# In-place weight conversion, more homes for weight blocks, and scores of three tiles in two row groups

## The chip, the cores and the metric

The kernel runs on one core of a Trainium2 chip. The metric is the device time of one execution in microseconds (us). Engines are TensorE (PE, with its weight loads PEld), VectorE (DVE), ScalarE (ACT), GpSimd (POOL) and SyncE (SP, which issues the DMAs).

## The reference

Local attention with a distance bias, followed by a gated channel mix. B, H, S, D = 4, 8, 768, 64; the model width is 512, the hidden width 1024.

```python
scores = scale * np.matmul(q, k.transpose(0, 1, 3, 2))
is_global = pos[None, :] < int(n_global)            # 8
is_local = (rel >= 0) & (rel < int(n_local))        # 96
dist = np.where(is_global & ~is_local, float(n_local), np.abs(rel))
scores = np.where(is_global | is_local, scores - slopes * dist, -1e9)
a = softmax(scores); x = a @ v                      # heads side by side: (4, 768, 512)
xk = mu_k * x + (1 - mu_k) * x_prev                 # xr likewise with mu_r
k = np.maximum(xk @ w_k, 0.0); v = k * k @ w_v
out = v / (1 + np.exp(-(xr @ w_r)))
```

The three weight matrices come as 64-bit floats; the rest as 32-bit floats.

## The kernel before, in words

**Tiles and steps.** The 3072 rows are 24 tiles of 128 queries, six for each batch. Step n does the scores of tile n, pair of heads by pair of heads (hp = 0 to 3), the transposes of tile n - 1 and the weighted sum over v of tile n - 2. A tile sees its own 128 keys and 128 earlier ones (the first tile of a batch only its own). Two tiles make a chunk of 256 rows; the channel mix of a chunk, an "FFN", is a generator whose pieces (`yield`) are dealt out between the pairs by `run_ffn`, five for each pair. FFN 0 is queued in step 3 with a budget of -17.5, so that its first matmuls stand in program order at that step's end.

**Scores.** Tiles 0 to 6 (`n < NATIVE`) use native 32-bit matmuls, later ones a high and a low part (L323, L324). A head has 64 rows. In the native tiles each query tile (`padded`, four buffers) has zeros in the other 64 rows, so that heads 0 to 3 (rows 0 to 63) and 4 to 7 (rows 64 to 127) go through all 128 rows of the array against `ring`, which holds the keys of both halves (L320 earlier keys, L321 own keys). The scores of one pair are in one PSUM buffer of a pool of two (`ps_s`). DVE adds the bias and takes the row's extreme (L332), ACT takes the exponential (L333), DVE sums and inverts (L339, L340), POOL scales (L343). Results lie in `room`, 12 slots.

**Weights.** There are 20 blocks of 128 x 512: 8 of w_k, 4 of w_r, 8 of w_v. A block is a DMA of 512 KB (L160), one multiplication on ACT or POOL by turns (L175, L173), and three integer passes on DVE (L176, L177, L178) which make 32-bit words of the two halves of a 64-bit number. The intermediate `a` has a place of its own, and the result goes into a `word` (pool `wl`, 21 buffers). The raw blocks lie in homes that others need later or earlier: w_k k=0 and k=1 in kk_hi and kk_lo, k=2 in xk_hi, k=3 in xr_hi, each for both column halves in turn; w_r and w_v in the three buffers `t4k`, with `a` in pool f2. kk_hi also holds the setup's temporary, and xk_hi, xr_hi, kk_hi receive the inputs (L429, L430) and the hidden values (L480) of FFN 0.

**FFN 0 and the others.** FFN 0 multiplies with the words as they are (`kp` L471, `z` L450, `vps` L507). For FFN 1 and later each word is split into a high part (`w_hi`, a copy on ACT or POOL) and a low part (DVE, L187 or L190), and each product has three matmuls (L441 to L443). `splits_ok` says how many blocks may be split, and one is split for each piece of FFN that is dealt.

**Order.** The program order is written out by hand in the loop over steps; after each pair a rule gives the number of weight loads and conversions that are due (`due`), and conversions are held behind the last score instructions of the pair before (`marks`, filled from `seen`). A planner then orders each engine's queue by program order and by its own simulated time; the queues are worked off in order.

Of the kernel before, what the change touches and what calls it, by code (L numbers as in the profile page):

```python
# [24 lines left out]
NATIVE = 7  # L25
MOVED = 9
# [7 lines left out]
def tile_biased_attention_channel_mix(ctx: ExitStack, tc: tile.TileContext, qT, kT, v, n_sizes, mu_kr, w_k, w_v, w_r, q_rows, k_rows, v_rows, slopes, out):  # L34
# [108 lines left out]
    w_steps = [(name, src, k, c) for name, src, kts, n in (("k", w_k, 4, DF), ("r", w_r, 4, DM), ("v", w_v, 8, DM)) for c in range(0, n, 512) for k in ((1, 2, 3, 0) if name == "k" else range(kts))]  # L143

    w_raw = {}

    def weight_load(i):
        name, src, k, c = w_steps[i]
        if name != "k":
            raw = p4k.tile([128, 512, 2], I32, tag="t4k", name=f"w64_{i}")  # L150
            a = f2_pool.tile([128, 512], I32, tag="f2", name=f"wa_{i}")
        elif k < 2:
            both = f_pool.tile([128, 2048], I32, tag=("kk_hi", "kk_lo")[k], name=f"w64_{i}")
            raw = both[:, 0:1024].rearrange("p (n w) -> p n w", w=2)
            a = both[:, 1024:1536]
        else:
            t = "xk" if k == 2 else "xr"
            raw = f_pool.tile([128, 512, 2], I32, tag=t + "_hi", name=f"w64_{i}")
            a = f_pool.tile([128, 512], I32, tag=t + "_lo", name=f"wa_{i}")
        nc.sync.dma_start(raw.rearrange("p n w -> p (n w)"), src[k * 128 : (k + 1) * 128, 2 * c : 2 * c + 1024])  # L160
        w_raw[i] = raw, a

    def weight_begin(i):
        name, src, k, c = w_steps[i]
        raw, a = w_raw.pop(i)
# [3 lines left out]

        if i % 2:
            pool.tensor_scalar(a.bitcast(F32), top.bitcast(F32), 2.0**-112, 1.0, op0=ALU.mult, op1=ALU.mult)  # L173
        else:
            act.mul(a.bitcast(F32), top.bitcast(F32), 2.0**-112)  # L175
        vec.tensor_scalar(a, a, 3, 0x7FFFFFF8, op0=ALU.logical_shift_left, op1=ALU.bitwise_and)  # L176
        vec.scalar_tensor_tensor(a, top, -0x80000000, a, op0=ALU.bitwise_and, op1=ALU.bitwise_or)  # L177
        vec.scalar_tensor_tensor(word, low, 29, a, op0=ALU.logical_shift_right, op1=ALU.bitwise_or)  # L178
# [58 lines left out]
    def load_tile(n):  # L237
        b, t = divmod(n, NT)
        s = state[n] = {}
        if n < NATIVE:  # L240
            qr, kr = padded[n % 4], ring[:, n % 4]
            for o, h in sides:
                nc.sync.dma_start(qr[o : o + 64, h : h + HH], qT[n, :, h : h + HH])
# [64 lines left out]
    def scores(n, hp):  # L308
# [5 lines left out]
        ps = ps_s.tile([128, 512], F32, name=f"s_{n}_{hp}", tag="s")  # L314
        for u in range(2):
            h = 2 * hp + u
            o = ps[:, u * 256 : u * 256 + w]
            if n < NATIVE:
                if t:
                    pe.matmul(o[:, 0:128], s["qr"][:, h, :], state[n - 1]["kr"][:, h % HH, :], start=True, stop=True)  # L320
                pe.matmul(o[:, w - 128 : w], s["qr"][:, h, :], s["kr"][:, h % HH, :], start=True, stop=True)  # L321
            else:
                pe.matmul(o, s["qh"][:, h, :], s["kw"][:, h, c0:256], start=True, stop=False)  # L323
                pe.matmul(o, s["ql"][:, h, :], s["kw"][:, h, c0:256], start=False, stop=True)  # L324
        if hp == 3 and n + 1 < NATIVE and (n + 1) % NT >= 2:
            vec.tensor_copy(s["kr"][:, :, 0:32], firsts)
        for u in range(2):
            h = 2 * hp + u
            o = ps[:, u * 256 : u * 256 + w]
            slot = 5 + (4 * (n - MOVED + 3) + 3 + hp) % 7 if n < MOVED - 2 else 8 + hp  # L330
            e = room[:, slot, 256 * u : 256 * u + 256]
            vec.tensor_tensor_reduce(out=e[:, :w], in0=o, in1=p[:, h, :], op0=ALU.add, op1=ALU.min, scale=-0.125, scalar=3.0e38, accum_out=s["nmax"][:, h : h + 1])  # L332
            seen["act"] = act.activation(e[:, :w], e[:, :w], AF.Exp, bias=s["nmax"][:, h : h + 1], scale=-1.0, accum_out=s["sum"][:, h : h + 1]).ins  # L333
            s["e"][h] = e
        if hp % 2 == 0:
            return
        h0, nh = 2 * hp - 2, 4
# [419 lines left out]
```

## Time and profile before

| | us |
|---|---|
| median of 3 runs | 490.45 (488.69 to 490.99) |
| the profiled execution | 487.47 |
| its span in the trace | 485.6 |
| PE busy | 471.2 |
| DVE busy | 379.2 |
| ACT busy | 280.1 |
| POOL busy | 254.3 |

A row of busy times is for one engine or one stretch. In a timeline, a line merges instructions of one kind: its start, its length, how many, and in brackets the idle time of the engine ahead of them with what released it. Matmuls overlap in the pipeline, so the distance between starts, not the length, tells what one occupies.

### The profile page before, as it was taken

What the parts mean: (1) busy time and instruction counts of PE and PEld (TensorE: products, weight loads), DVE (VectorE), ACT (ScalarE), POOL (GpSimd) and SP (SyncE); (2) the same over time, 40 slices, a digit from 0 to 9 for tenths busy, and PEclk for the clock granted to TensorE, in tenths of its full rate; (3) what the DMA queues carried; (4) which work ended last, traced back from release to release, by engine and by line L of the source; (5) the groups of instructions that cost most, each with busy time, mean ns of one, the idle gap of its engine ahead of it and who ended that gap; (6) DMA issues with size and microseconds to landing.
All of it is one profiled execution on the core that took longest, in us unless ns stands there. A gap on an engine that the chain in (4) does not pass through costs nothing.

```text
span 485.6 us, 9692 instructions
## 1 busy us (share of the span) xinstructions
PE 471.2 (97%) x3300; PEld 405.5 (84%) x3300; DVE 379.2 (78%) x921; ACT 280.1 (58%) x654; POOL 254.3 (52%) x396
## 2 busy tenths in 40 slices
PE   7997999999999999999999999999999999999996
PEld 6786855597898898898898898898898898898985
DVE  6899599898867978978988978978978968846321
ACT  5996345445658746645856746745748648544220
POOL 7677446735847535746646655637646635403000
PEclk9998999999999999999999999999999999999999
DMA  6994457331442464783685786683775655430001
GB/s 170 300 328 126 131 173 179 87 115 45 107 111 67 138 198 137 213 269 110 178 237 167 208 245 174 207 238 130 196 210 186 196 171 167 141 126 12 33 2 48
DMA packets 42279, 76.20 MB, mean 157 GB/s; under 512 B 5616, under 2 KB 23280, under 8 KB 42224
## 3 DMA queue, kind: packets, MB, share of 16 engines
q1 hardware_dynamic: 42080, 75.52, 52.6%
q8 instruction: 28, 0.46, 0.4%
q14 instruction: 27, 0.22, 0.2%
q10 hardware_dynamic: 144, 0.00, 0.0%
HBM read 54.53 MB, written 20.97 MB: 155 GB/s over the span
## 4 chain that ended last, share of the span: by engine, by line
PE 78%; DVE 10%; DMA 5%; issue 2%; POOL 2%; ACT 2%; SPq 0%; DVEq 0%; POOLq 0%
PE vps L442 8%; PE vps L441 8%; PE vps L443 8%; PE kp L441 8%; PE kp L443 8%; PE kp L442 8%; PE av L401 7%; PE z L441 4%; PE z L442 4%; PE s L323 4%; PE z L443 4%; PE s L324 3%; DMA w<-in_w_v_dram 2%; PE t L380 1%; DMA ring<-in_kT_dram 1%
## 5 line engine op out<-in xcount | busy, mean ns | idle before, releaser
L343 POOL TENSOR_SCALAR room<-room,r 128x256 f32<-128x256 f32 (+1 forms) x192 | 108.0, 579 | 131.7 <-DVE r L340 65.4
L333 ACT ACTIVATE room<-room,nmax 128x256 f32<-128x256 f32 (+1 forms) x192 | 92.8, 484 | 90.2 <-DVE nmax L332 84.2
L441 PE MATMUL kp<-xk_hi,wk_hi 128*128 128x256 f32 x352 | 99.5, 283 | 0.7 <-ACT xk_hi L420 0.7
L443 PE MATMUL kp<-xk_hi,wk_lo 128*128 128x256 f32 x352 | 98.6, 280 | 0.0
L442 PE MATMUL kp<-xk_lo,wk_hi 128*128 128x256 f32 x352 | 98.3, 279 | 0.0
L332 DVE CUSTOM_DVE_ANT_0 room<-s,pat 128x256 f32<-128x256 f32 (+1 forms) x192 | 68.5, 388 | 3.9 <-PE s L321 2.5
L442 PE MATMUL vps<-wv_lo,kk_hi 128*128 128x512 f32 (+1 forms) x184 | 70.9, 385 | 0.0
L441 PE MATMUL vps<-wv_hi,kk_hi 128*128 128x512 f32 (+1 forms) x184 | 70.8, 385 | 0.0
L443 PE MATMUL vps<-wv_hi,kk_lo 128*128 128x512 f32 (+1 forms) x184 | 70.5, 383 | 0.0
L441 PEld LDWEIGHTS kp<-xk_hi,wk_hi 128*128 128x128 f32 x352 | 66.8, 190 | 1.8 <-ACT xk_hi L420 1.0
L442 PEld LDWEIGHTS kp<-xk_lo,wk_hi 128*128 128x128 f32 x352 | 66.0, 187 | 0.8 <-issue 0.2
L443 PEld LDWEIGHTS kp<-xk_hi,wk_lo 128*128 128x128 f32 x352 | 66.0, 188 | 0.0
L354 DVE STREAM_TRANSPOSE room<-room 128x512 f32<-128x512 f32 x52 | 36.0, 702 | 17.9 <-POOL room L343 17.9
L486 DVE TENSOR_TENSOR kk_lo<-kk,kk_hi 128x512 fp32r<-128x512 f32 x44 | 34.1, 775 | 14.2 <-ACT kk_hi L485 12.8
L485 ACT CAST kk_hi<-kk 128x512 fp32r<-128x512 f32 x44 | 27.1, 616 | 25.9 <-DVE kk L484 25.9
L484 DVE TENSOR_TENSOR kk<-kp,kk 128x512 f32<-128x512 f32 x44 | 30.1, 685 | 14.8 <-ACT kk L478 14.8
L443 PEld LDWEIGHTS vps<-wv_hi,kk_lo 128*128 128x128 f32 x184 | 34.6, 188 | 7.4
L401 PE MATMUL av<-room,va 128*64 128x128 f32 x608 | 40.4, 278 | 0.0
L441 PEld LDWEIGHTS vps<-wv_hi,kk_hi 128*128 128x128 f32 x184 | 34.7, 188 | 6.4
L401 PEld LDWEIGHTS av<-room,va 128*64 128x64 f32 x608 | 34.2, 136 | 6.7 <-issue 4.1
L442 PEld LDWEIGHTS vps<-wv_lo,kk_hi 128*128 128x128 f32 x184 | 34.5, 188 | 6.1
L323 PE MATMUL s<-kw,qh 128*128 128x256 f32 (+1 forms) x136 | 37.1, 295 | 0.9 <-DVE kw L298 0.9
(118 smaller groups left out, 1029.4 us busy)
## 6 DMA issues: line engine op xcount, KB each, us to landing
moved<-room SPq DMA_DIRECT2D x26, 512.0 KB, 3.7
room<-moved SPq DMA_DIRECT2D x104, 128.0 KB, 3.1
kraw<-in_kT_dram SPq DMA_DIRECT2D x36, 256.0 KB, 4.1
qraw<-in_qT_dram SPq DMA_DIRECT2D x34, 256.0 KB, 4.1
out_dram<-sig SPq DMA_DIRECT2D x23, 256.0 KB, 3.7
va<-in_v_dram SPq DMA_DIRECT2D x21, 256.0 KB, 4.0
w<-in_w_k_dram SPq DMA_DIRECT2D x8, 512.0 KB, 6.7
w<-in_w_v_dram SPq DMA_DIRECT2D x8, 512.0 KB, 4.8
```

What stands on the lines that cost most here:

```text
L323: pe.matmul(o, s["qh"][:, h, :], s["kw"][:, h, c0:256], start=True, stop=False)
L332: vec.tensor_tensor_reduce(out=e[:, :w], in0=o, in1=p[:, h, :], op0=ALU.add, op1=ALU.min, scale=-0.125, scalar=3.0e38, accum_out=s["nmax"] ...
L333: seen["act"] = act.activation(e[:, :w], e[:, :w], AF.Exp, bias=s["nmax"][:, h : h + 1], scale=-1.0, accum_out=s["sum"][:, h : h + 1]).ins
L343: seen["pool"] = pool.tensor_scalar(e[:, :w], e[:, :w], r[:, u : u + 1], 1.0, op0=ALU.mult, op1=ALU.mult).ins
L354: vec.transpose(dst, src.rearrange("p u (g b j) -> p (u g) b j", b=4, j=32))
L401: pe.matmul(o, vt[:, h * 64 : (h + 1) * 64], g, start=k == 0, stop=k == nb - 1)
L441: pe.matmul(o, sh, mh, start=first, stop=False)
L442: pe.matmul(o, sh, ml, start=False, stop=False)
L443: pe.matmul(o, sl, mh, start=False, stop=last)
L484: vec.tensor_mul(kk, pv, kk)
L485: act.copy(kkh[:, 2 * fp : 2 * fp + 2, :], kk)
L486: vec.tensor_sub(kkl[:, 2 * fp : 2 * fp + 2, :], kk, kkh[:, 2 * fp : 2 * fp + 2, :])
```

## The change

A weight block is converted in its `word` and needs no intermediate. The raw blocks get a list of homes: w_k one each (xk_hi, xr_hi, xk_lo, xr_lo, and two each in kk_hi and kk_lo), w_r and w_v in t4k three times, xk_lo and xr_lo, twice over, and the last two in kk_lo. Loads and conversions are due by a table for each slot (4 x step + hp) in place of the rule, most of them later; the order of w_k's blocks is plain; `seen` stays empty, so conversions are no longer held behind scores. Splits are allowed from the second half of FFN 0's first `vps` on, not from `kp` on.

The native scores of tiles 4, 5 and 6 load the query heads of both halves into the same columns (no zeros), and multiply with 64 rows: pairs j and j + 2 (j = 0, 1), one in rows 0 to 63 and one in rows 64 to 127, matmul by matmul in turn, into two PSUM buffers, in the places of hp 0 and 2; nothing at hp 1 and 3. Sums are inverted for these four heads. Tiles 5 to 8 use other slots of `room`.

```diff
+PADDED = 4
-    w_steps = [... for k in ((1, 2, 3, 0) if name == "k" else range(kts))]
+    w_steps = [... for k in range(kts)]
+    w_due = ((2, 3, 4, 5, 6, 6, 7, 7, 8, 8, 9, 9, 10, 11, 12, 13, 14, 16, 18, 20, 20, 20, 20, 20), (0, 1, 2, 3, 4, 4, 5, 5, 6, 6, 7, 7, 8, 8, 9, 10, 11, 12, 14, 16, 18, 20, 20, 20))
     def weight_load(i):
         name, src, k, c = w_steps[i]
-        if name != "k":
+        home = w_homes[i]
+        if home == "t4k":
             raw = p4k.tile([128, 512, 2], I32, tag="t4k", name=f"w64_{i}")
-            a = f2_pool.tile([128, 512], I32, tag="f2", name=f"wa_{i}")
...
+        elif home[0] == "x":
+            raw = f_pool.tile([128, 512, 2], I32, tag=home, name=f"w64_{i}")
+        else:
+            if home in w_both:
+                raw = w_both.pop(home)[:, 1]
+            else:
+                w_both[home] = f_pool.tile([128, 2, 512, 2], I32, tag=home, name=f"w64_{i}")
+                raw = w_both[home][:, 0]
...
+    w_homes = ["xk_hi", "xr_hi", "xk_lo", "xr_lo", "kk_hi", "kk_hi", "kk_lo", "kk_lo"] + 2 * ["t4k", "t4k", "t4k", "xk_lo", "xr_lo"] + ["kk_lo", "kk_lo"]
...
-            act.mul(a.bitcast(F32), top.bitcast(F32), 2.0**-112)
-        vec.tensor_scalar(a, a, 3, 0x7FFFFFF8, ...)
-        vec.scalar_tensor_tensor(a, top, -0x80000000, a, ...)
-        vec.scalar_tensor_tensor(word, low, 29, a, ...)
+            act.mul(word.bitcast(F32), top.bitcast(F32), 2.0**-112)
+        vec.tensor_scalar(word, word, 3, 0x7FFFFFF8, ...)
+        vec.scalar_tensor_tensor(word, top, -0x80000000, word, ...)
+        vec.scalar_tensor_tensor(word, low, 29, word, ...)
...
-                nc.sync.dma_start(qr[o : o + 64, h : h + HH], qT[n, :, h : h + HH])
+                c = h if n < PADDED else 0
+                nc.sync.dma_start(qr[o : o + 64, c : c + HH], qT[n, :, h : h + HH])
...
+        elif hp % 2:
+            return
+        else:
+            j = hp // 2
+            units = [(i, ps_s.tile([128, 512], F32, name=f"s_{n}_{i}", tag="s")) for i in (j, j + 2)]
+            for u in range(2):
+                for k in (0, 1) if t else (1,):
+                    for i, ps in units:
+                        x = slice(64 * (i // 2), 64 * (i // 2) + 64)
+                        h = 2 * j + u
+                        keys = (s if k else state[n - 1])["kr"]
+                        pe.matmul(ps[:, u * 256 + 128 * k - c0 : u * 256 + 128 * k - c0 + 128], s["qr"][x, h, :], keys[x, h, :], start=True, stop=True)
...
-            slot = 5 + (4 * (n - MOVED + 3) + 3 + hp) % 7 if n < MOVED - 2 else 8 + hp
+                slot = 5 + (4 * (n - MOVED + 4) + 3 + i) % 7 if n < MOVED - 3 else i + (4 if n < MOVED and (MOVED - n) % 2 else 8)
-            seen["act"] = act.activation(...).ins
+                act.activation(...)
...
-        et = room[:, (4 * n + hp) % 5 if n < MOVED - 1 else hp]
+        et = room[:, (4 * n + hp) % 5 if n < MOVED - 4 else hp]
...
                 vec.tensor_mul(kk_all[:, 2 * fp : 2 * fp + 2, :], pv, kk)
-                if fp % 2:
-                    splits_ok[0] = 2 * fp + 2
...
-        if first:
-            splits_ok[0] = 12
...
-                        if i:
-                            splits_ok[0] = 13 + f
+                        if i or f > 3:
+                            splits_ok[0] = 13 + f if i else 12
...
-            due = [min(8, 2 + max(x, -1) * 4 // 3) if x < 6 else 8 + (x - 5) * 6 // 7 for x in (4 * step + hp, 4 * step + hp - 2)]
-            weights_load(due[0])
-            weights_go(due[1])
+            slot = 4 * step + hp
+            weights_load(w_due[0][min(slot, 23)])
+            weights_go(w_due[1][min(slot, 23)])
```

## Rows read from the trace of the kernel before

**Rows 1.** Part 1 of the page: busy time, share of the span, instructions.

```profile
PE 471.2 (97%) x3300; PEld 405.5 (84%) x3300; DVE 379.2 (78%) x921; ACT 280.1 (58%) x654; POOL 254.3 (52%) x396
```

**Rows 2.** Busy time by stretch (length, engines, PEclk, DMA share, GB/s).

```profile
18.00:24.00 6.00, 4.79 (x40) 3.45 (x40) 6.00 (x22) 5.04 (x15) 3.58 (x5) 1.00 1.06 262
...
30.00:36.00 6.00, 4.98 (x40) 4.19 (x38) 6.00 (x23) 5.84 (x19) 5.17 (x8) 1.00 1.04 297
36.00:42.00 6.00, 4.19 (x48) 3.67 (x48) 5.12 (x16) 4.39 (x14) 4.77 (x8) 1.00 0.99 270
42.00:48.00 6.00, 4.68 (x18) 3.98 (x19) 5.86 (x14) 3.87 (x11) 4.45 (x7) 0.72 0.02 6
...
54.00:60.00 6.00, 6.00 (x33) 5.33 (x32) 1.99 (x4) 1.64 (x3) 2.83 (x5) 1.00 0.55 175
...
84.00:90.00 6.00, 5.10 (x24) 2.34 (x23) 5.23 (x10) 3.43 (x7) 2.44 (x3) 1.00 0.04 9
...
132.00:200.00 68.00, 68.00 (x513) 60.90 (x512) 54.55 (x134) 45.63 (x99) 39.14 (x61) 1.00 0.49 142
```

**Rows 3.** Timeline of PE around the first matmuls of FFN 0.

```profile
43.32 1.22 PE L471 MATMUL kp<-xk,word 128*128 128x256 f32 x2 [2.72 <-DVE xk L430]
44.33 1.06 PE L380 MATMUL t<-ident,room 128*128 128x128 f32 x4
45.19 1.06 PE L471 MATMUL kp<-xk,word 128*128 128x256 f32 x2
46.04 0.93 PE L380 MATMUL t<-ident,room 128*128 128x128 f32 x4
46.81 6.21 PE L471 MATMUL kp<-xk,word 128*128 128x256 f32 x28
```

**Rows 4.** Timelines of ACT and of DVE ahead of FFN 0.

```profile
27.92 0.59 ACT L409 COPY x<-av 128x512 f32<-128x512 f32 x1 [0.16 <-PE av L401]
...
40.49 1.71 ACT L429 ACTIVATE xk<-x,mus 128x256 f32<-128x256 f32 x4 [1.61 <-DVE r L340]
...
39.64 0.68 DVE L178 SCALAR_TENSOR_TENSOR word<-w,wa 128x512 int32<-128x512 int32 x1
...
42.14 0.48 DVE L286 COPY early<-ring 128x128 f32<-128x128 f32 x1 [1.02 <-DMA ring<-in_kT_dram]
42.54 0.72 DVE L430 SCALAR_TENSOR_TENSOR xk<-x,mus,xk 128x256 f32<-128x256 f32 x1
```

**Rows 5.** Groups of DVE instructions, the three passes: busy us, mean ns, idle before.

```profile
L177 DVE SCALAR_TENSOR_TENSOR wa<-w,wa 128x512 int32<-128x512 int32 x16 | 11.7, 749 | 0.0
L178 DVE SCALAR_TENSOR_TENSOR word<-w,wa 128x512 int32<-128x512 int32 x16 | 11.5, 731 | 0.0
...
L176 DVE TENSOR_SCALAR wa<-wa 128x512 int32<-128x512 int32 x16 | 7.4, 470 | 6.8 <-POOL wa L173 3.6 <-ACT wa L175 3.1
```

**Rows 6.** Timeline of PE: native scores, weighted sums, and the way between kinds.

```profile
31.70 0.39 PE L321 MATMUL s<-ring,qz 128*128 128x128 f32 x2
31.92 0.39 PE L320 MATMUL s<-ring,qz 128*128 128x128 f32 x2
...
66.57 0.40 PE L401 MATMUL av<-room,va 128*64 128x128 f32 x4
66.79 0.38 PE L401 MATMUL av<-room,early 128*64 128x128 f32 x2
67.00 0.38 PE L401 MATMUL av<-room,va 128*64 128x128 f32 x2
...
93.55 0.28 PE L442 MATMUL kp<-xk_lo,wk_hi 128*128 128x256 f32 x1
93.67 0.28 PE L443 MATMUL kp<-xk_hi,wk_lo 128*128 128x256 f32 x1
93.88 1.15 PE L401 MATMUL av<-room,va 128*64 128x128 f32 x16
94.95 0.66 PE L380 MATMUL t<-ident,room 128*128 128x128 f32 x4
```

More of the change, by code (lines that the diff above doesn't have):

```diff
@@ L313, in scores @@
         p = pat if t else pat0
[L314 to L322, printed above, removed]
+        if not PADDED <= n < NATIVE:
+            ps = ps_s.tile([128, 512], F32, name=f"s_{n}_{hp}", tag="s")
+            for u in range(2):
+                h = 2 * hp + u
+                o = ps[:, u * 256 : u * 256 + w]
+                if n < PADDED:
+                    if t:
+                        pe.matmul(o[:, 0:128], s["qr"][:, h, :], state[n - 1]["kr"][:, h % HH, :], start=True, stop=True)
+                    pe.matmul(o[:, w - 128 : w], s["qr"][:, h, :], s["kr"][:, h % HH, :], start=True, stop=True)
+                    continue
@@ L335, in scores @@
-        if hp % 2 == 0:
-            return
-        h0, nh = 2 * hp - 2, 4
-        r = s_pool.tile([128, nh], F32, name=f"r_{n}_{hp}", tag="r", bufs=8)
-        vec.tensor_scalar(r, s["sum"][:, h0 : h0 + nh], 1.0e-9, None, op0=ALU.add)
-        seen["vec"] = vec.reciprocal(r, r).ins
-        for u in range(nh):
-            e = s["e"][h0 + u]
-            seen["pool"] = pool.tensor_scalar(e[:, :w], e[:, :w], r[:, u : u + 1], 1.0, op0=ALU.mult, op1=ALU.mult).ins
+            units = ((hp, ps),)
+        elif hp % 2:
[3 more added lines that the diff above has]
+            units = [(i, ps_s.tile([128, 512], F32, name=f"s_{n}_{i}", tag="s")) for i in (j, j + 2)]
+            for u in range(2):
+                for k in (0, 1) if t else (1,):
[4 more added lines that the diff above has]
+                        pe.matmul(ps[:, u * 256 + 128 * k - c0 : u * 256 + 128 * k - c0 + 128], s["qr"][x, h, :], keys[x, h, :], start=True, stop=True)
@@ new lines, in scores @@
+        if hp >= (2 if n >= PADDED else 3) and n + 1 < NATIVE and (n + 1) % NT >= 2:
+            vec.tensor_copy(s["kr"][:, :, 0:32], firsts)
+        for i, ps in units:
+            for u in range(2):
+                h = 2 * i + u
+                o = ps[:, u * 256 : u * 256 + w]
+                slot = 5 + (4 * (n - MOVED + 4) + 3 + i) % 7 if n < MOVED - 3 else i + (4 if n < MOVED and (MOVED - n) % 2 else 8)
+                e = room[:, slot, 256 * u : 256 * u + 256]
+                vec.tensor_tensor_reduce(out=e[:, :w], in0=o, in1=p[:, h, :], op0=ALU.add, op1=ALU.min, scale=-0.125, scalar=3.0e38, accum_out=s["nmax"][:, h : h + 1])
+                act.activation(e[:, :w], e[:, :w], AF.Exp, bias=s["nmax"][:, h : h + 1], scale=-1.0, accum_out=s["sum"][:, h : h + 1])
+                s["e"][h] = e
@@ new lines, in scores @@
+        rows = PADDED <= n < NATIVE
+        if not rows and hp % 2 == 0:
+            return
+        r = s_pool.tile([128, 4], F32, name=f"r_{n}_{hp}", tag="r", bufs=8)
+        if rows:
+            heads = (2 * j, 2 * j + 1, 2 * j + 4, 2 * j + 5)
+            total = s["sum"].rearrange("p (a j u) -> p j a u", a=2, j=2)[:, j]
+        else:
+            heads = range(2 * hp - 2, 2 * hp + 2)
+            total = s["sum"][:, 2 * hp - 2 : 2 * hp + 2].rearrange("p (a u) -> p a u", a=2)
+        vec.tensor_scalar(r.rearrange("p (a u) -> p a u", a=2), total, 1.0e-9, None, op0=ALU.add)
@@ L345, in turn @@
+        vec.reciprocal(r, r)
+        for i, h in enumerate(heads):
+            e = s["e"][h]
+            pool.tensor_scalar(e[:, :w], e[:, :w], r[:, i : i + 1], 1.0, op0=ALU.mult, op1=ALU.mult)
     def turn(n, hp):
```

30 lines of the change are left out of this document (8 added, 22 removed).

## The prediction

> **What bounds the kernel now.** I first read the busy line of the page: TensorE (PE) has 471.2 of 485.6 us, 97%, and no other engine is near that [rows 1]. The table of busy times by stretch then says where the other 14.4 us lie. From 132 us on PE is full (68.00 of 68.00) while VectorE (DVE) is not [rows 2]; there the time is a count of matmuls, and the change doesn't touch any of them. What can move lies ahead of 132 us. PE lacks 1.02 us in 30 to 36, 1.81 in 36 to 42, 1.32 in 42 to 48, 1.21 in 18 to 24 and 0.90 in 84 to 90 [rows 2]. In 42 to 48 the granted clock is 0.72 on the mean: part of it ran at 1.2 GHz in place of 2.4 GHz, right after PE had stood idle for 2.72 us [rows 2, 3]. What that costs is read off the starts: from 43.32 to 46.81 PE got through 4 records of kp and 8 of t; at the full level 28 records of kp take 6.21 us, some 0.216 each after the first [rows 3], and a record of t as much as a native one below, 0.11 [rows 6], so 1.74 us of work took 3.49. The clock costs 1.75 us.
>
> Why PE waits there is in the timelines of ACT and DVE [rows 4]. PE's first matmul of FFN 0 (L471) waits for DVE's xk (L430), and that for ACT's xk (L429). ACT had its input, x from av, at 28.5, yet started at 40.49 after 1.61 us idle. The view lays this to DVE's reciprocal; that is only what DVE finished last. The code has a better cause: xk's tile has the tag xk_hi, and that home holds the raw block w_k k=2, twice, so xk may not be written until the second block's last reader, L178, is through. An L178 runs from 39.64 to 40.32, and ACT starts at 40.49. Then DVE, in order, stands for 1.02 us before L286, which needs the keys of tile 6, with xk behind it. So the start of FFN 0 hangs on a home, and DVE, which must clear it, is full: 22.98 of the 24 us in 18 to 24 and 30 to 48 [rows 2].
>
> **Homes and in-place conversion.** No instruction is removed: 20 blocks keep a pass on ACT or POOL and three on DVE, 0.470 + 0.749 + 0.731 = 1.95 us each [rows 5]. All eight w_k blocks now have homes of their own, and xk_hi and xr_hi are used once, by the first two. xk may then be written when x is there: 28.5, plus 1.71 for ACT, plus about four DVE passes at 0.72 (partly under ACT) gives 33, ten microseconds before 43.3. PE can't gain ten: tiles 4 and 5 do part of their work in that time. It can gain its idle time, 1.02 + 1.81 + 1.32 = 4.15, and the 1.75 of the clock, as an idle of 2.72 us no longer stands ahead: 5.9 at most. What is late next is DVE. In 18 to 24, with DVE full and no home in the way, PE still lost 1.21 us; I leave as much for this stretch. Term: 5.9 - 1.2 = **4.7 us**, bounds 0 (DVE gives nothing back) and 5.9.
>
> **w_r, w_v and low parts later.** By slot 12 (step 3, first pair) the old rule has 12 conversions due, the new table 8: 4 x 1.95 = 7.8 us less for DVE before FFN 0. That pays for the four xk and four xr passes, some 5 us, that move forward with FFN 0. The work comes back behind 45 us, where DVE has cover: in 54 to 60 it was busy for 1.99 of 6 [rows 2]. Low parts (an estimate: one DVE pass of L178's size, 0.731 us [rows 5], for each of 20 blocks) move out of FFN 0's first half to its last twelve steps and into FFN 1. If that cover is gone, FFN 1's first matmuls wait: 84 to 90 already lost 0.90. I take **0.4 us** here as more homes bring w_v sooner, bounds -0.9 and 0.9. On SP's queue the same 20 loads of 512 KB are issued, later, so the q, k and v loads pass earlier. The wait at L286 (1.02) may go; it is inside the 4.15 and isn't counted twice. Nothing for 18 to 24, bounds -1.2 and 1.2: the conversions lose their order behind the scores (the dictionary of marks stays empty now).
>
> **Scores in two row groups.** A native matmul leaves two records, and 0.22 us lie between the starts of one pair and of the next: 0.111 per record [rows 6]. Tiles 4 and 5 have 16 matmuls each, tile 6 has 8: 40 matmuls, 80 records, 8.9 us. Two heads in the two halves of the array at once have not run here. The nearest row is av, whose output sits in two column halves of 64: four records take 0.22 (66.57 to 66.79), 0.055 each, but two take 0.21 (66.79 to 67.00), 0.105 each [rows 6]. I read the first as two halves running together and the second as one half alone. It isn't free: into av 0.21 lie between starts (93.67 to 93.88) where 0.12 lie one record before, 0.09 more, and the 16 records of av then take 1.07 until the next kind starts, in place of 0.88, 0.19 more [rows 6]. A visit costs 0.28. A unit (two pairs of heads of one tile) of tiles 4 and 5 has 16 records: 16 x 0.055 + 0.28 = 1.16 for 1.78, a gain of 0.62. A unit of tile 6 has 8: 0.72 for 0.89, 0.17. Two units each: 1.24, 1.24 and 0.34. Tiles 5 and 6 lie where PE will be the bound: 1.6 in full. Tile 4 lies at 31 to 37, where PE will still wait for DVE some of the time, and a unit needs both PSUM buffers of the scores, which DVE frees one after the other: half, 0.6. Term: **2.2 us**, bounds -1.7 (six visits paid for nothing) and 2.8.
>
> The Trainium skill, page "TensorEngine Tiling (Array Packing)", section Key Properties, says that a change of tiling mode drains the engine, and that different tiles load and multiply in parallel. By that rule, the trace agrees on the drain (0.09 us more into av); on the parallel loads of row groups no run here shows it. Its page "TensorE: Matmul & The Clock Gate", section LDWEIGHTS, speaks against this part: a load's time goes by columns and not by rows, so a load of 64 rows is as long as one of 128. If loads then also took turns, this term would be -1.7 and not 2.2.
>
> The other edits (room's slots for tiles 6 to 8, the four-head sum taken as a strided view) change no count of work; I cost them at nothing, under DVE's and POOL's other work from 90 us on.
>
> **Sum.** 4.7 + 0.4 + 2.2 = 7.3 us. The profiled execution took 487.47 (its span is 485.6), so 480.2 for its like; the median of the three runs is 490.45, 3 us above, and the forecast stands against that: **483.1 us**.
>
> **Rivals.** (a) The row groups take turns. For it: no row shows two loads of 128 columns side by side, and av's blocks are half as wide, which alone could explain 0.055. Against it: the same av instruction shows 0.105 too. Time: 4.7 + 0.4 - 1.7 = 3.4, so 487.0. (b) DVE takes the place of the home: FFN 0 starts early but then waits for w_k's second half and w_r, as DVE is 96% full up to 48. The first term drops to about 1, and the second to 0: 1 + 1.6 = 2.6, 487.8. Against it: four blocks fewer are due. (c) Slower. With the marks empty, conversions may stand on DVE ahead of the scores of tiles 1 to 4 whenever their block has landed, and with more homes more have. Each costs 1.95. FFN 0 would start at 33 + 1.95 b for b blocks that overtake; from b = 5.3 nothing is left of the ten microseconds, and from b = 6.4 the scores' gain is eaten too. At 8 blocks it starts 5.3 us late, less 2.2 and with 0.9 lost at FFN 1: 4.0 more, 494.5. Against it: loads are issued in the order of due times, and with the DMA share at 0.99 to 1.06 in 18 to 42 [rows 2] the blocks can't all have landed early. (d) The homes were not the cause, and xk waited for DVE's order all along: the first term is 0, 2.6 remain, 487.8.
>
> **How the numbers follow.** Forecast 0.55; (a) 0.15; (b) and (d) together 0.18; (c) 0.12. All bounds taken well give 5.9 + 1.2 + 0.9 + 2.8 = 10.8, 479.6, and as the lengths of matmul records overlap their neighbours' and may hide some idle time, the low end is 477.5. The high end, 490.5, takes in (a), (b) and (d) with their misses and leaves (c) out. About 0.5% is what a measurement of this kernel can tell from no change, that is below 488.0 or above 492.9. Faster: 0.54 from the forecast, 0.11 from (a), 0.09 from (b) and (d), 0.74. Slower: 0.01 from (b) and (d), 0.09 from (c), 0.10. The same: the rest, 0.16.
>
> **What would show it.** In the changed profile L471 starts near 33 to 36, and not after an idle of over 2 us; PEclk has no 0.7 in 42 to 48. ACT's L429 starts within 2 us of L409's second copy. Score records of tile 5 and 6 come at under 0.07 each. If they come at 0.11, (a) holds; if PE's idle time in 30 to 60 is laid to L178, (b); if tile 3's scores end much after 30, (c). The stretch from 132 us on should keep its length. I am wrong if FFN 0 starts before 36 and the end doesn't follow.

## The result, and the profile after

The changed kernel took **482.77 us** (median of 4 runs, 482.41 to 483.20), the kernel before 490.72 on the same chip (4 runs, 488.69 to 491.60); the ratio is 0.9864, interval 0.9818 to 0.9911. The forecast was 483.1. Run again ten times in a later batch, the changed kernel took 483.62 (482.09 to 487.84), the kernel before 488.57: 0.9903 (0.9873 to 0.9933). The profiled execution took 482.42 us with a span of 480.6, against 487.47 and 485.6, which is 5.05 us less and not the 7.3 of the sum. The sign and the size are right; the terms, below, are right in part only. Luck of the clock is in it: the four executions have a mean granted clock of 0.9975, the ten later ones 0.9937, and in the profiled one PE spends nothing at 1.2 GHz between 10 us and its end.

The busy line of the page after answers to [rows 1]: PE has lost 2.9 us of work, DVE has gained 1.4.

```profile
PE 468.3 (97%) x3300; PEld 402.7 (84%) x3300; DVE 380.6 (79%) x921; ACT 283.0 (59%) x656; POOL 255.5 (53%) x396
```

Busy time by stretch, after (columns as in [rows 2]):

```profile
18.00:24.00 6.00, 4.87 (x38) 3.42 (x37) 6.00 (x20) 6.00 (x19) 3.43 (x5) 1.00 1.03 274
30.00:36.00 6.00, 3.12 (x20) 1.99 (x20) 6.00 (x19) 6.00 (x18) 6.00 (x8) 1.00 1.04 300
36.00:42.00 6.00, 5.98 (x39) 4.89 (x38) 6.00 (x17) 4.69 (x13) 3.04 (x6) 1.00 1.03 342
42.00:48.00 6.00, 6.00 (x63) 5.43 (x63) 6.00 (x17) 3.67 (x11) 4.36 (x6) 1.00 0.93 281
...
72.00:78.00 6.00, 5.35 (x20) 2.32 (x20) 6.00 (x17) 4.18 (x10) 6.00 (x9) 1.00 0.75 117
84.00:90.00 6.00, 5.60 (x47) 3.95 (x47) 5.93 (x17) 2.55 (x9) 3.72 (x5) 1.00 0.81 208
96.00:102.00 6.00, 5.21 (x47) 4.86 (x46) 5.11 (x17) 2.95 (x11) 1.26 (x4) 1.00 0.08 26
114.00:120.00 6.00, 6.00 (x34) 5.00 (x33) 4.90 (x12) 5.94 (x11) 6.00 (x12) 1.00 0.32 90
132.00:200.00 68.00, 68.00 (x486) 60.34 (x486) 56.60 (x139) 45.81 (x100) 37.99 (x63) 1.00 0.51 143
```

PE is now full in 36 to 48, at a PEclk of 1.00. But in 30 to 36 it is busy for 3.12 us only, where it had 4.98 [rows 2]: the idle time has gone down and moved forward, not away. And this is one execution. In a second profile of the same kernel (again, below) PE lacks 3.27 us in 30 to 36, and the granted clock falls to 1.2 GHz there; its stretch 36 to 42:

```profile
36.00:42.00 6.00, 5.72 (x24) 4.44 (x23) 4.02 (x9) 4.35 (x12) 3.44 (x5) 0.52 1.03 357
```

Three smaller losses stand where there were none or less: 0.65 in 72 to 78, 0.40 in 84 to 90 (0.90 before), 0.79 in 96 to 102. From 132 us on PE is full as before, and from the 48th record of FFN 1's vps to PE's end both kernels take 349.9 us. All of the change lies ahead of that.

One stretch of before that the prediction didn't read loses a stall: there PE lacked 0.89 us in 114 to 120, in front of the first scores with a high and a low part. The timeline of PE before, at that place:

```profile
117.87 0.39 PE L323 MATMUL s<-kw,qh 128*128 128x256 f32 x1 [0.89 <-DVE kw L298]
```

Now the start of FFN 0. The lines have moved: x is copied at L433 (was L409), xk is L453 (L429), kp is L495 (L471), a transpose L404 (L380), POOL's scaling L367 (L343), the scores with 64 rows L341. The timeline of PE after, which answers to [rows 3]:

```profile
32.74 0.38 PE L404 MATMUL t<-ident,room 128*128 128x128 f32 x2
34.49 0.44 PE L404 MATMUL t<-ident,room 128*128 128x128 f32 x2 [1.36 <-POOL room L367]
35.62 0.90 PE L404 MATMUL t<-ident,room 128*128 128x128 f32 x4 [0.70 <-POOL room L367]
36.35 1.46 PE L495 MATMUL kp<-xk,word 128*128 128x256 f32 x6
37.65 0.38 PE L404 MATMUL t<-ident,room 128*128 128x128 f32 x2
37.96 1.71 PE L341 MATMUL s<-ring,qz 64*128 64x128 f32 x16
39.60 0.70 PE L495 MATMUL kp<-xk,word 128*128 128x256 f32 x2
```

FFN 0 starts at 36.35 in place of 43.32, and no idle time stands right ahead of it. The timeline of ACT after, for [rows 4]:

```profile
28.94 0.59 ACT L433 COPY x<-av 128x512 f32<-128x512 f32 x1
29.56 1.31 ACT L453 ACTIVATE xk<-x,mus 128x256 f32<-128x256 f32 x3
```

xk follows x at once, at 29.56 and not at 40.49: it did hang on its home. What PE waits for now is POOL. The timeline of POOL after:

```profile
26.01 0.77 POOL L175 TENSOR_SCALAR word<-w 128x512 f32<-128x512 f32 x1 [1.68 <-DMA w<-in_w_k_dram]
27.62 1.06 POOL L217 TENSOR_SCALAR wk_hi<-word 128x512 fp32r<-128x512 f32 x1 [0.84 <-DVE r L364]
28.66 3.31 POOL L367 TENSOR_SCALAR room<-room,r 128x256 f32<-128x256 f32 x4
31.95 1.08 POOL L217 TENSOR_SCALAR wk_hi<-word 128x512 fp32r<-128x512 f32 x1
33.00 0.81 POOL L175 TENSOR_SCALAR word<-w 128x512 f32<-128x512 f32 x1
33.79 2.23 POOL L367 TENSOR_SCALAR room<-room,r 128x256 f32<-128x256 f32 x3
```

Ahead of the scaling of tile 3's later heads (33.79) stand a copy of a high part, which no one needs before FFN 1 at about 84, and a multiplication of a w_k block. Ahead of those POOL stood 1.68 us for another w_k block to land (26.01), with the scaling behind it. The waits of PE from 24 to 131 us, after (total, times, longest), say the same:

```profile
PE t L404 <- POOL room L367: 3.6, 4, 1.4
PE kp L465 <- DVE kk L506: 0.8, 1, 0.8
PE vps L527 <- DVE word L180: 0.5, 1, 0.5
```

### The profile page after: what moved, and what is told of

The parts are those of the page before. It is cut to its first block, busy times and chain, and to the rows that moved or that the text cites. A ratio compares the mean times of both kernels' runs of the same rounds, so it can differ in the third digit from the quotient of the medians.

```text
span 480.6 us, 9646 instructions
## 1 busy us (share of the span) xinstructions
PE 468.3 (97%) x3300; PEld 402.7 (84%) x3300; DVE 380.6 (79%) x921; ACT 283.0 (59%) x656; POOL 255.5 (53%) x396
## 4 chain that ended last, share of the span: by engine, by line
PE 84%; DVE 8%; POOL 2%; issue 2%; DMA 2%; SPq 0%; ACT 0%; POOLq 0%; DVEq 0%
PE vps L466 9%; PE vps L465 9%; PE vps L467 8%; PE kp L465 8%; PE av L425 8%; PE kp L467 8%; PE kp L466 8%; PE z L465 4%; PE z L466 4%; PE z L467 4%; PE s L327 4%; PE s L328 3%; PE t L404 2%; POOL room L367 2%; PE s L325 2%
## 5 line engine op out<-in xcount | busy, mean ns | idle before, releaser
L367 POOL TENSOR_SCALAR room<-room,r 128x256 f32<-128x256 f32 (+1 forms) x192 | 110.2, 591 | 141.7 <-DVE r L364 72.9
```

Source lines behind the costliest of these rows:

```text
L367: pool.tensor_scalar(e[:, :w], e[:, :w], r[:, i : i + 1], 1.0, op0=ALU.mult, op1=ALU.mult)
```

## The experiments

Time is a median beside its ratio to the kernel before on the same chip, with the 95% interval. Milestones are starts in the one profiled execution of each kernel. "FFN 0" is its first kp record, "half of kp" the 33rd. The first four ran on one chip, then four more, then three, then one.

### The change taken apart: scores or weights alone

w_only keeps all of the change but the 64-row scores:

```diff
-PADDED = 4
+PADDED = 7
```

> The changed kernel with the scores of tiles 4 to 6 as before (zeros, 128 rows); homes, table, splits and room slots stay changed. In the changed kernel's trace the six units of 64 rows take 1.64, 1.64, 1.09, 1.64, 0.64 and about 0.64 us, 7.3, and some 0.09 each on the way in, against 8.9 for 80 records at 0.111. Theory (the weights carry the gain, the rows give about 1): 483.8 us, FFN 0 starts within 1 us of 36.4. Rival (the two-at-once scores free other engines or the pair slots and carry half): 486 to 487.

485.72 us, 0.9946 (0.9921 to 0.9971), between the two expectations. FFN 0 starts at 37.32. The weights' part alone gives about 2.6 us (0.0054 of 488.56). Its profiled execution has an idle of 2.5 us ahead of FFN 0, and then the clock falls; the stretch 36 to 42 of w_only:

```profile
36.00:42.00 6.00, 5.53 (x30) 4.69 (x31) 5.23 (x15) 4.29 (x12) 3.53 (x5) 0.72 1.04 332
```

rows_only keeps the scores, with their slots of room, and has all of the weights' part as before (homes, the place of `a`, the rule, the marks, the splits):

```diff
-    w_homes = ["xk_hi", "xr_hi", "xk_lo", "xr_lo", ...]
...
-            weights_load(w_due[0][min(slot, 23)])
-            weights_go(w_due[1][min(slot, 23)])
+            weights_load(due[0])
+            weights_go(due[1])
```

> The changed kernel with the weights of before: homes, intermediate, rule of due times, marks and splits; only the scores of tiles 4 to 6 (and the room slots) are changed. Theory: the rows give some 1 us and FFN 0 still waits for its home, starting at 42 to 44: 489 to 490. Rival: 486 to 487 with FFN 0 earlier.

491.19 us, 1.0066 (1.0042 to 1.0091): slower than before. FFN 0 starts at 43.10, as before, and its half of kp is 1.9 us earlier (52.28 for 54.19). The profiled execution (487.86) is the fastest of the ten, so it doesn't show the loss of the median. It shows that FFN 0's vps then waits, by the waits of PE in rows_only:

```profile
PE vps L530 <- DVE word L179: 2.9, 2, 2.2
```

The last w_v blocks are issued at 73.23 and 77.07, when their homes come free, and are not converted in time for a vps that starts 2.4 us earlier (70.65 for 73.04). The last record of vps starts at 95.16 (before 92.30), and 3.4 us from 89.5 on, behind the longer wait, are at 1.2 GHz, as are 3.4 us from 38.3 on. In this execution the scores' gain is lost at vps, for want of weights. What makes the other nine slower is in no trace; their granted clock is lower (0.9877 on the mean of ten, the kernel before 0.9952).

homes_only has in-place conversion and the homes, and the old rule, marks, splits and scores:

```diff
-PADDED = 4
+PADDED = 7
...
-            weights_load(w_due[0][min(slot, 23)])
+            weights_load(due[0])
...
+                seen["act"] = act.activation(...).ins
...
+                if fp % 2:
+                    splits_ok[0] = 2 * fp + 2
```

> In-place conversion and the list of homes alone: rule of due times, marks, splits and scores as before. Theory (the home of xk was what FFN 0 waited for): FFN 0 starts at 34 to 38 and the time is 484 to 486. Rival (b, d: DVE's order and load are what it waited for, and the later table is what frees it): FFN 0 starts after 40, 488 to 490.

487.93 us, 0.9972 (0.9949 to 0.9996), about 1.4 us by the ratio. FFN 0 does start early, at 37.70, but kp's half is reached at 57.92, later than before. The timelines of PE and of ACT in homes_only show why:

```profile
49.41 2.00 PE L425 MATMUL av<-room,early 128*64 128x128 f32 x16 [4.42 <-ACT room L351]
```

```profile
48.10 0.70 ACT L177 ACTIVATE word<-w 128x512 f32<-128x512 f32 x1 [4.07 <-DMA w<-in_w_v_dram]
```

The wait is longer than the 2.72 us that were removed. It is laid to the exponentials of tile 4, but ACT wasn't busy with them: it stood 4.07 us at the multiplication of the first w_v block, with the exponentials behind it. That block was issued at 36.63 and landed 11.5 us later; the old rule has its conversion due at slot 13, the new table at slot 18. But due, below, has the old rule too and no such wait, so the rule alone doesn't make it. Besides, 6.8 us from 25.2 on and 3.4 from 49.1 on are at 1.2 GHz. Homes free the start; they don't put the queues behind it in order.

### The parts put back one at a time

again is the changed kernel itself, for the spread.

> The changed kernel once more, for a comparison on the same chip as the three below: 482 to 483.5, a ratio of 0.985 to 0.99.

483.62 us, 0.9903 (0.9873 to 0.9933). In its profiled execution PE waits for the same things, but for POOL 2.5 us at the longest in place of 1.4, and 6.8 us from 35.0 on are granted 1.2 GHz. The mean granted clock of its ten runs goes from 0.986 (487.84 us) to 0.998 (482.09).

due puts the old rule in place of the table:

```diff
-            slot = 4 * step + hp
-            weights_load(w_due[0][min(slot, 23)])
-            weights_go(w_due[1][min(slot, 23)])
+            due = [min(8, 2 + max(x, -1) * 4 // 3) if x < 6 else 8 + (x - 5) * 6 // 7 for x in (4 * step + hp, 4 * step + hp - 2)]
+            weights_load(due[0])
+            weights_go(due[1])
```

> The changed kernel with the old rule of due times; homes, no marks, splits and rows stay changed. By slot 12 the rule asks for 12 conversions in place of 8, 4 x 1.95 us more for DVE before FFN 0. Theory (DVE, full from 18 to 84, sets the pace, so the later table carries a good part): the second half of kp starts at 53 or later in place of 49.9, 485 to 487. Rival (the planner moves conversions by its own time whatever is due): 482.8.

486.89 us, 0.9973 (0.9947 to 0.9999): 3.3 us above again. FFN 0 starts at 36.49, as after, but kp's half comes at 54.32 (49.94 after, 52.91 in again), and 10.2 us from 35.1 on are at 1.2 GHz, right behind one idle of 2.8 us, where again has 6.8:

```profile
PE t L404 <- POOL room L367: 2.8, 1, 2.8
```

The loss is not one of waiting, as far as this trace goes: between 12 and 132 us PE lacks 5.2 us here and 6.0 in again. The 3.4 us more at 1.2 GHz, half of them lost, are enough for the 1.4 by which kp's half comes later than in again.

marks fills `seen` again, so that conversions are held behind the scores:

```diff
-                act.activation(...)
+                seen["act"] = act.activation(...).ins
...
-        vec.reciprocal(r, r)
+        seen["vec"] = vec.reciprocal(r, r).ins
...
+            seen["pool"] = pool.tensor_scalar(...).ins
```

> The changed kernel with conversions held behind the last score instructions again. In the changed kernel the scores of tile 3 end at 32.6 in place of 30.3. Theory (conversions that overtake on DVE cost this; rival c of the prediction in a small size): tile 3 ends by 31, FFN 0 starts at 34 to 35, 481 to 482. Rival (holding them back makes w_k late): 484 or more, with PE waiting for words.

490.86 us, 1.0044 (1.0022 to 1.0067), 7.2 us above again: put back alone, this small part undoes everything. The start is not late: FFN 0 begins at 35.93 and kp's half is at 50.14, though 3.4 us from 36.2 on are at 1.2 GHz. The loss is in the second half of vps, in marks' busy time by stretch:

```profile
84.00:90.00 6.00, 0.75 (x7) 0.54 (x5) 4.56 (x9) 0.98 (x4) 4.83 (x5) 0.78 0.67 161
```

and in PE's waits there:

```profile
PE vps L527 <- DVE word L180: 6.4, 1, 6.4
```

What held the words is in the timeline of POOL in marks:

```profile
82.40 4.81 POOL L367 TENSOR_SCALAR room<-room,r 128x256 f32<-128x256 f32 x4 [3.19 <-DVE r L364]
87.18 0.64 POOL L175 TENSOR_SCALAR word<-w 128x512 f32<-128x512 f32 x1
```

The multiplication of a w_v block stands behind a scaling of scores (82.40), as the mark has it, and that one waits for DVE. The words come 6.4 us after PE has asked for them.

splits allows splits where the kernel before did:

```diff
                 vec.tensor_mul(kk_all[:, 2 * fp : 2 * fp + 2, :], pv, kk)
+                if fp % 2:
+                    splits_ok[0] = 2 * fp + 2
```

> The changed kernel with the low parts allowed from FFN 0's kp on, as before. Theory (20 low parts at some 0.7 us, put ahead of w_v's conversions on a full DVE, make vps wait): PE waits for words in vps grow, 484 to 486. Rival (planner and word buffers decide when they run): 482.8.

487.72 us, 0.9966 (0.9934 to 0.9997), 4.1 above again. FFN 0 starts at 39.40. The timeline of POOL in splits:

```profile
35.74 0.65 POOL L175 TENSOR_SCALAR word<-w 128x512 f32<-128x512 f32 x1 [1.78 <-DMA w<-in_w_k_dram]
36.37 2.50 POOL L367 TENSOR_SCALAR room<-room,r 128x256 f32<-128x256 f32 x3
```

Here the multiplication ahead of tile 3's scaling stands 1.78 us for its block, and PE's transposes with it. The edit only says earlier in the program, in FFN 0's kp, that blocks may be split; the planner's order at 28 to 36, ahead of kp, is another one with it. vps's second half is longer as well (10.05 us for 6.98).

apart gives the intermediate a place of its own in f2 again:

```diff
+        a = f2_pool.tile([128, 512], I32, tag="f2", name=f"wa_{i}")
-        vec.tensor_scalar(word, word, 3, 0x7FFFFFF8, ...)
+        vec.tensor_scalar(a, a, 3, 0x7FFFFFF8, ...)
```

> The changed kernel with the intermediate of each conversion in a place of its own again (pool f2, four buffers, shared with the hidden values and gates of FFN 0), so that only the words are converted out of place; homes, table, splits, rows stay. It asks what in-place conversion itself gives. Theory (little: the homes were the bound, not the intermediate): 482.5 to 484. Rival (with f2 shared, conversions and FFN 0's values wait for each other): 485 to 487, with waits for kk or sig in front of L175 and L177.

489.00 us, 1.0002 (0.9977 to 1.0027): nothing is left of the gain. The waits of PE in apart, from 24 to 131 us (its profiled execution is the slowest of the ten):

```profile
PE t L405 <- POOL room L368: 4.6, 3, 3.4
PE vps L528 <- DVE word L181: 3.2, 1, 3.2
```

The second is a wait for words late in FFN 0, as in rows_only; f2 also holds FFN 0's kk and sig, and `a` must wait for them. POOL stands 2.6 us for DVE's kk ahead of one multiplication (62.98), and the last four multiplications start at 77.49 to 87.24, in the changed kernel at 58.47 to 65.73. In-place conversion, which saves no instruction, is needed for the rest to pay.

### The two row groups by themselves

The changed kernel writes the 64-row matmuls of the two halves in turn, but they don't run that way everywhere. Timelines of PE after, a unit of tile 5, the other unit of tile 5, and a unit of tile 6:

```profile
65.50 1.16 PE L341 MATMUL s<-ring,qz 64*128 64x128 f32 x16
66.59 0.70 PE L474 MATMUL z<-word,xr 128*128 128x512 f32 x1
...
77.17 1.72 PE L341 MATMUL s<-ring,qz 64*128 64x128 f32 x16
78.81 0.70 PE L527 MATMUL vps<-word,kk 128*128 128x512 f32 x1
...
90.91 0.71 PE L341 MATMUL s<-ring,qz 64*128 64x128 f32 x8
91.55 0.39 PE L465 MATMUL kp<-xk_hi,wk_hi 128*128 128x256 f32 x1
```

16 records take 1.09 us in one unit and 1.64 in another. The single records tell them apart: from 65.50 on they start in twos, 0.006 us between the two and 0.11 from one two to the next. In the two units of tile 4, of 1.64 each, five records of the one half start first, 0.11 apart, and five stand alone at the end: PE's queue has another order there. In the slow unit of tile 5 two records of the one half start, then 0.38 us pass, and then the halves alternate. There the second half waits for its PSUM buffer, which DVE frees with its last read of the scores before, at 77.61 (timeline of DVE after):

```profile
77.53 0.08 DVE L350 DVE_READ_ACCUMULATOR2_ANT nmax<- 128x1 f32 x1
```

alt makes each 64-row matmul follow the one before it in program order:

```diff
+                        with ExitStack() as turns:
+                            if last:
+                                turns.enter_context(tc.issue_after(last[-1]))
+                            last.append(pe.matmul(...).ins)
```

> The changed kernel with an order edge from each 64-row matmul of a unit to the next, so that the two halves take turns in PE's queue in each unit. In the changed kernel three units of 16 records took 1.64 us as five records of one half ran alone first; one took 1.09, its records in pairs 0.006 apart. Theory: all four take 1.1 and, as PE is full from 36 on, the time falls by up to 1.6: 481.2. Rival (DVE sets the pace up to 84, PE's gain turns into waiting): 482.8, no change, with 0.5 more idle at each of the three units.

482.57 us, 0.9870 (0.9844 to 0.9895). Three of the four units of 16 records now take 1.1 to 1.2 us; tile 5's second, which waits for its buffer, is as slow as it was (timeline of PE in alt):

```profile
78.64 1.72 PE L345 MATMUL s<-ring,qz 64*128 64x128 f32 x16
80.28 0.70 PE L531 MATMUL vps<-word,kk 128*128 128x512 f32 x1
```

That is some 1.0 us less of PE's work and no time that can be told from that of the changed kernel. Beside w_only on the same chip (0.9946, 0.9921 to 0.9971) it shows what the scores are worth on top of the weights: 0.76%, 3.7 us, of which a part is the clock (below). Refuted is that row groups take turns.

### What paces the start: DVE, POOL or the clock

light leaves out one of the three DVE passes of all 20 blocks:

```diff
-        vec.scalar_tensor_tensor(word, top, -0x80000000, word, op0=ALU.bitwise_and, op1=ALU.bitwise_or)
```

> The changed kernel without the second of the three integer passes of each conversion (the sign is left out, so words of negative weights come out positive): 20 passes, some 14 us of DVE less, nothing else changed. It asks whether DVE, full from 18 to 84 in the changed kernel, sets the pace of the first 100 us. Theory: FFN 0 starts 2 us or more earlier, PE's idle time in 30 to 102 (4.7 us) falls to under 2, 478 to 480. Rival (PE and its waits on transposes and POOL set it): 482 to 483.

481.82 us, 0.9897 (0.9848 to 0.9946): by the ratio 0.3 us better than again, which can't be told from none. DVE is busy for 368.7 us, 11.9 less than after, 8.9 of it ahead of 90 us. FFN 0 even starts later, at 39.59, since the planner now puts tile 4's first scores ahead of it. But PE's idle time did what the theory said: in 30 to 102 it is 1.68 us for 4.74, and the waits for POOL's scaling are gone. The longest of the waits of PE in light, from 24 to 131 us:

```profile
PE s L340 <- DVE nmax L349: 1.4, 2, 1.0
```

The time did not follow, as 6.8 us from 37.6 on are at 1.2 GHz, behind an idle of 0.99; the stretch 36 to 42 of light:

```profile
36.00:42.00 6.00, 5.53 (x24) 4.77 (x25) 5.82 (x18) 6.00 (x20) 4.31 (x6) 0.64 1.04 341
```

So what DVE has to do stands behind PE's waits for POOL. It isn't shown whether by DVE's time itself or by the planner's order, which changes with it: POOL's copies (34.43, 36.69) now stand behind tile 3's scaling, not ahead of it.

fill gives PE four matmuls with zeros ahead of each pair of transposes of tiles 2 and 3:

```diff
+            if u == 0 and n in (2, 3):
+                for _ in range(4):
+                    pe.matmul(pt[:, 0:256], zeros[:, 0:128], zeros, start=True, stop=True)
```

> The changed kernel with four matmuls of zeros (128x256, 16 bit, 0.107 us each at the full level) put ahead of each of the eight transposing pairs of tiles 2 and 3, where PE waits for POOL between 22 and 36: 32 matmuls, 3.4 us, results overwritten. It asks what the clock costs in the usual execution: of the ten runs of the changed kernel on one chip, seven had a mean granted clock of 0.995 or less and the times spread from 482.1 to 487.8. Theory: PE isn't the bound there, the filling keeps the clock at its full level, and the median falls to 481.5 to 482.5 with a spread under 2. Rival: the filling delays transposes and costs 1 to 3 us: 484 to 486.

486.73 us, 0.9988 (0.9960 to 1.0016), by the ratios 4.1 above again. Of the 32 matmuls with zeros, 16 ran ahead of the wait (23.6 to 29.3) and 16 behind it, at 40.0 to 62.8, where PE is full; none ran in it. The timeline of PE in fill:

```profile
36.41 1.36 PE L407 MATMUL t<-ident,room 128*128 128x128 f32 x4 [3.13 <-POOL room L367]
```

PE stood for 3.13 us just the same, and from 36.5 on 3.4 us are at 1.2 GHz. So the run doesn't say what a filled wait would give.

hi_late holds the copies of the high parts behind tile 4's last scores on ACT and POOL (`late` holds those):

```diff
-        (act.copy if i % 4 < 2 else pool_copy)(hi, word)
+        with ExitStack() as behind:
+            for ins in late.values():
+                behind.enter_context(tc.issue_after(ins))
+            (act.copy if i % 4 < 2 else pool_copy)(hi, word)
```

> The changed kernel, with the copies of the weights' high parts (on ACT and POOL) held behind the last score instructions of tile 4 on those engines. In the changed kernel POOL has two of these copies, 1.06 us each, at 27.62 and 31.95, ahead of tile 3's scaling, for which PE waits in 30 to 36, where it stands idle 2.88 us; the high parts are first needed by FFN 1, about 84. Theory (POOL's order makes that idle time): the idle time in 30 to 36 falls by 1 to 2 us, FFN 0 starts at 34 to 35.5, and the time is 481 to 482.5. Rival (the copies only bunch later, or the planner's other places change with them, as with the other variants): PE waits as long at another place, on POOL or ACT in 36 to 90, and the time is 483.5 to 487.

490.62 us, 1.0032 (0.9995 to 1.0068). Both came true, the theory at its place and the rival for the time, worse than it said. FFN 0 starts at 34.59, and POOL's order was indeed the cause of PE's wait. The waits of PE in hi_late:

```profile
PE vps L535 <- DVE word L180: 5.7, 1, 5.7
PE av L433 <- DMA early<-in_v_dram: 3.2, 1, 3.2
PE t L412 <- POOL room L373: 1.1, 4, 0.4
```

The wait for the scaling is down from 3.6 to 1.1. But the load of early values is issued at 36.99 and not at 34.15, behind loads of w_r, and PE stands 3.2 us for it. Then the eight copies that were held run in one block on POOL, 67.66 to 74.86, with a multiplication of a w_v block behind them (74.83); so the words come late, and PE stands 5.7 us at 81. In each of the two the level falls (at 41.2 and 85.6) and stays at 1.2 GHz for 6.8 us.

How much of all these differences is the clock? The low level costs an execution at most (1 - its mean granted clock) x its span, less where PE stood idle at it. The table takes that estimate off each execution; the column of as measured is the difference of the medians to the kernel before on the same chip.

| run | mean granted clock (kernel before) | as measured, us | clock taken off, us |
|---|---|---|---|
| w_only | 0.9937 (0.9952) | -2.8 | -3.5 |
| rows_only | 0.9877 (0.9952) | 2.6 | -0.7 |
| homes_only | 0.9909 (0.9952) | -0.6 | -3.4 |
| alt | 0.9960 (0.9952) | -6.0 | -5.3 |
| again | 0.9937 (0.9944) | -4.9 | -5.0 |
| due | 0.9884 (0.9944) | -1.7 | -4.7 |
| marks | 0.9897 (0.9944) | 2.3 | 0.1 |
| splits | 0.9910 (0.9944) | -0.8 | -2.9 |
| light | 0.9892 (0.9949) | -6.3 | -8.2 |
| fill | 0.9927 (0.9949) | -1.4 | -2.1 |
| apart | 0.9916 (0.9949) | 0.8 | -0.6 |
| hi_late | 0.9892 (0.9949) | 1.6 | -1.4 |

Each number of the last column is good to 1 to 1.5 us. By it due loses nothing, homes alone give what the whole of the weights' part gives, and the rows alone don't slow the kernel; marks, apart, hi_late, fill and splits keep a loss of 2 to 5 us to again, and light gains 3. Why one order of work meets the low level more often than another is in no run.

## Why the prediction was right, and where it wasn't

**Homes and in-place conversion, 4.7 us: the mechanism right, 3.0 measured.** The cause read from [rows 4] is confirmed: xk comes 0.03 us behind x. Rival (d) is out. "FFN 0 starts 33 to 36" came to 36.35, "no idle of over 2 us" to 1.36, "no 0.7 PEclk in 42 to 48" to 1.00 in this execution, and ACT's xk within 0.6 us of L433's second copy. The bound was 4.15 of idle and 1.75 of clock in 30 to 48, 5.9; after, the same stretch lacks 2.88 + 0.02 = 2.90, so 3.0 are gained, 1.25 of idle time and 1.75 of clock. But in again's profile the stretch lacks 3.55 and has 6.8 us at 1.2 GHz, so there it gains nothing, and over ten executions the mean granted clock is 0.9937 for 0.9944 before. So the 1.75, which the prediction took as won with the idle of 2.72, is luck of one execution. The failing step is "what is late next is DVE", sized by 18 to 24 as 1.2: in front of PE POOL was late next, 2.9 (3.3 in again). It was so in 18 to 24 already. The timeline of PE before:

```profile
21.54 0.44 PE L380 MATMUL t<-ident,room 128*128 128x128 f32 x2 [0.79 <-POOL room L343]
```

That scaling stood behind a multiplication (20.02) for which POOL had waited 3.04 us for its w_k block to land. With that line and POOL's row in [rows 2], busy for 5.17 in 30 to 36, POOL's queue should have been read. What makes it late is not settled: hi_late takes most of the wait away by POOL's order, light all of it by DVE's work. "Tile 3's scores end much after 30" came out for rival (c), at 32.6, and the time did not follow it.

The term was also given to the wrong parts. Homes alone give 1.4 us (homes_only). The table, the marks left out, the splits moved and the conversion in place, each put back, take 3.3 to 7.2 us away as measured. With the clock taken off that is 0.3 for the table, 2 for the splits, 4 for the place and 5 for the marks, and homes_only gives 3.4. Those amounts add up to far more than the gain, so they are no shares of it: marks and apart each make PE stand once more, at vps (6.4 and 3.2 us), and splits longer at the old place (3.1 for 2.5 in again). That the table is needed isn't shown.

**Weights later, 0.4 us: 0.9 lost.** The prediction's cover behind 45 us is not there: DVE is full in 72 to 78 and nearly so in 84 to 90. PE lacks 0.65 + 0.40 + 0.79 = 1.84 in three stretches between 72 and 102, for 0.90 before (in again 0.40 + 0.76 up to 103). That is the lower bound given, "FFN 1's first matmuls wait". Against it stands a stall that the prediction did not read, 0.89 ahead of 117.87. No other run has it in full; w_only keeps 0.24, and homes_only, with the old scores too, nothing, so it isn't the 64 rows that remove it.

**Loss of the marks, 0 for 18 to 24: right there, wrong as a place.** That stretch has 1.13 of idle time for 1.21. But the marks decide in vps, 60 us later, by 6.4 us, and so the sign of rival (c) was the wrong way round: marks left empty help, because they let the words of w_v come in time. The prediction saw only who might be overtaken, and not who would be held.

**Two row groups, 2.2 us: the rate right, the order not.** The rate of 0.055 for a record, read from av [rows 6], is the rate of units that alternate: 1.09 and 0.09 for the way in for 16 (1.16 forecast), 0.64 and 0.09 for 8 (0.72). Rival (a) is out. By the rule of the Trainium skill, "TensorEngine Tiling (Array Packing)", Key Properties, that different tiles load and multiply in parallel, the trace now agrees, 0.006 us apart; the Trainium skill's page "TensorE: Matmul & The Clock Gate", section LDWEIGHTS, which the prediction held against this part, doesn't lead to turns here. But three of four units of 16 did not alternate from their start, so the six units take 3 x 1.64 + 1.09 + 2 x 0.64 = 7.3 and some 0.5 for ways in, for 8.9 of native scores: 1.1 in place of 2.2. The step that fails is "matmul by matmul in turn": the code says it, but PE's queue doesn't keep it in tile 4, and in tile 5 the second half's buffer comes late once, the condition that the prediction named for tile 4 alone.

In time the scores seem worth more than that: w_only stands 2.1 us above again and 3.7 above alt, each relative to before. With the clock taken off w_only stands 1.5 above again and 1.8 above alt, near the 1.1 that the units give in the changed kernel and the 2.0 that they give in alt.

**The sum.** By the profiled executions PE's end moved by 5.07 us: 3.0 from 30 to 48, 1.1 from the score units, 0.9 from the stall ahead of 117.87 and 1.4 from the weighted sums, less 0.9 in 72 to 102 and 0.6 at the start; 0.2 are left. The prediction has no term for the weighted sums: between 60 and 100 us their 64 records occupy 5.5 us in eight visits before and 4.1 in two after, so most of the price of a visit, 0.28 in the prediction, was saved six times. With the intermediate in f2 they are split too (rows_only and apart, 5.6 in six visits), and in the other runs with in-place conversion (hi_late aside) they take 3.9 to 4.1 in two; why is in no run. At the start the first score records of the changed kernel come 0.21 apart, twice as far as before, so its next ones start at 9.99 for 9.36. The forecast gave 7.3. The median of 482.77 falls on 483.1 by luck in part: this batch had the kernel before at 490.72 and executions with a high granted clock; in the later batch the difference was 4.9 (0.97%). With the clock taken off, 3.5 of that are the weights' part (w_only, and 3.4 by homes_only) and 1.5 the scores; the forecast had 5.1 and 2.2. **Rival (b)** is out in its form: kp doesn't wait for w_k's words. But DVE can't be put aside: with one pass less on DVE, PE's idle time in 30 to 102 goes from 4.74 to 1.68 (light). The stretch from 132 on kept its length. **The slots of `room`**, costed at nothing, change for tiles 0 to 8 and not only for those named; every variant keeps them, so no run tests them alone.

## What to carry to other kernels

A home held by a late reader is found where an operation's input is there and its engine free, and yet it starts only behind another engine's last pass over that buffer; moving it buys no more than the time to the next late engine, so read the busy row of every engine in that stretch, POOL's too. An edit of a planned order is to be priced at the place where the moved work is needed, not where it stood: here marks and high parts changed waits 40 to 60 us away. Two variants are to be compared by their granted clocks before their times: here that turned the worth of homes and of the table around. Two row groups pay only where the halves alternate from the first record, which takes the queue's order and both buffers, and which the records must show, whatever the code says.

## What the runs showed of the hardware that was not expected

One kernel, with one set of queues, spends different times at 1.2 GHz from one execution to the next. After an idle of 1.36 us at 33 the profiled execution of the changed kernel kept 2.4 GHz; in again, with 2.5 us of idle at the same place, 6.8 us followed at 1.2 GHz. Elsewhere, too, the level fell behind or in PE's idle times: 2.5 us before 3.4 us (w_only), 2.8 before 10.2 (due), 3.1 before 3.4 (fill), and in the course of 3.1 and 6.4 us of idle time, for 6.8 each (splits, marks). But the length of one idle doesn't tell it: in light 6.8 us followed idles of 0.99 at the longest, in alt 3.4 us at 25.2 followed 0.79 and 0.40, and in alt an idle of 2.32 up to 36.8 was followed by none. Where PE has work all the while, half of such a stretch is lost (an estimate), so that 2.5 us of waiting cost up to 5.9 in all. In due the 10.2 us are worth up to 5.1, more than the 4.7 that the homes were forecast to give.

Two 64-row matmuls in different row groups start 0.006 us apart and together take 0.11 us; a single 64-row matmul takes 0.11 as well. The way into them costs 0.1 us (four transposes from 64.92, at 0.11 each, end at 65.36, and the scores start at 65.50), the way out another 0.1 (last start 66.39, next kind 66.59).
